# Joint attention products, FFN columns in two halves and a weight conversion divided anew between VectorE and GpSimd

## The chip, the cores and the metric

The kernel runs on one core of a Trainium2 chip. A core has a matrix engine (TensorE), three engines for elementwise work (VectorE, ScalarE, GpSimd; the profile calls them DVE, ACT and POOL), a queue engine that issues most of the transfers (SyncE, SP), and 16 DMA engines. SBUF is the core's working memory, PSUM the memory that TensorE writes to; both have 128 partitions. The metric is the time of one execution on the device in microseconds. Without the change it is 1402.33 us, the median of three runs (1402.2 to 1406.92).

## The reference

Two parts follow each other. The first is an attention that keeps only scores close to the row's maximum; the second a bilinear feed-forward layer (FFN).

```python
# q, k, v: (8, 8, 576, 64) float32; tau = 0.02
scores = q @ k.T / sqrt(64)
thresh = max(scores, axis=-1) - tau
scores = where(scores >= thresh, scores, -1e9)
attn = exp(scores - max(scores)); attn /= attn.sum(-1) + 1e-9
x = (attn @ v) -> (8 * 576, 8 * 64)       # 4608 tokens of 512 numbers
# w_a, w_b: (512, 1536), w_out: (1536, 512), handed over as float64
out = ((x @ w_a) * (x @ w_b)) @ w_out      # float32
```

The three weight matrices arrive as 8-byte floats. The chip computes here in 4-byte floats, so the kernel has to convert them itself.

## The kernel before

**Attention.** Two heads of one batch form a pair; there are 32 pairs, four to a batch, with the first head in partitions 0 to 63 and the second in 64 to 127. A pair's 576 query rows are four units of 128 rows and a remainder of 64; the remainders of two pairs make a unit of their own, so there are 144 units. The main loop (L1117) passes once per unit: such a pass is called a *slot*, with number g, and the first 16 or so differ from the rest. In slot g the kernel computes the scores of unit g on TensorE (`scores`, L404), takes the row maximum (L411) and the threshold (L412) on VectorE, the exponentials on ScalarE (`weigh`, L431 and L432), then on VectorE the *mask*: one instruction that compares, multiplies and sums (L435). The weights must then be turned, keys into partitions. The first eight units (`BY_PE`) are turned on TensorE by a product with a diagonal matrix (`turn_pe`, L483), which also divides by the row sum; ScalarE and VectorE copy the result out of PSUM (L485, L486). Later units are divided by ScalarE (L454), transposed in blocks by VectorE (`turn_blocks`, L502) and regrouped through DRAM by transfers (L144). The product with v (`product`, L546) follows two slots later for the first eight units (`weighted_unit`) and in wider parts for later ones. The first eight units belong to the four pairs of batch 0: units 0 to 3 are the first 128 rows of pairs 0 to 3, units 4 to 7 their second 128 rows.

`product` makes, for one pair, four quarter tiles of 64x64 in `pv`, one per combination of head and half of the columns, with 64 columns moving at a time. `settle` copies them into the tile xT, where partitions hold the 128 features of a pair: one copy by ScalarE (L553), two by VectorE (L554). `exchange` then makes xS on GpSimd (L569), which is xT with the two partition halves swapped, since the FFN's weights are stored so that both are read.

**Weights.** 36 pieces of 128x512 weights are loaded as pairs of 32-bit words (`load_weights`, L271) and converted over the first 16 slots, two or three a slot (`early`, L1113: three in slots 4 to 9). Per piece: ScalarE takes the absolute value of the upper word into the final place (`top`, L298) and prepares the lower word as a number near 2 (`low`, L299); GpSimd clamps `top` (L305); one slot later VectorE puts the sign bit of the upper word into `low` (L311) and shifts `top` left by three (L319); GpSimd adds both as integers (L324). `convert_rest(g, k)` does the last three steps for the k-th piece of slot g - 1, with k = 0 ahead of `weigh`, 1 and 2 near the end of the slot.

**FFN.** The tokens form 18 blocks of 256. `ffn` is a generator that gives out matmuls (L854 and L990 while weights are converted; later a scheme with fewer products, L750 and L920). `advance(cols)` draws from it until that many columns are issued; how many per slot is set by `pace` from fixed shares and from the backlog. Up to slot 8 all of a slot's FFN columns are issued at one place, behind `turn_pe`; from slot 9 on they are issued in four portions.

**Order.** Nothing is reordered: `keep_order` keeps each engine's instructions in the order in which the program issues them. All PSUM tiles come from one pool of four (`banks`), so a new tile waits until the oldest is free; a score tile is free when its mask (L435) is done. The loads of weights use a few rooms in turn and wait for one to be free, and for the last matmul issued before them (`behind`).

Of the kernel before, what the change touches and what calls it, by code (L numbers as in the profile page):

```python
# [23 lines left out]
BY_PE = 8  # L24
# [30 lines left out]
def kernel(  # L55
# [246 lines left out]
    def convert_clamp(n):  # L302
        if n in stages:
            top = pieces[n][0]
            nc.gpsimd.tensor_scalar(top, top, float_of(0x47EFFFFF), float_of(0x38000000),  # L305
                                    op0=ALU.min, op1=ALU.max)

    def convert_sign(n):
        if n in stages:
            low, hi = stages[n].bitcast(U32), raws.pop(n)[:, :, 1]  # L310
            nc.vector.scalar_tensor_tensor(out=low, in0=hi, scalar=0x80000000, in1=low,  # L311
                                           op0=ALU.bitwise_and, op1=ALU.bitwise_or)
            if n in taken:
                extra.append(taken.pop(n))

    def convert_shift(n):
        if n in stages:
            top = pieces[n][0].bitcast(U32)
            nc.vector.tensor_scalar(top, top, 3, None, op0=ALU.logical_shift_left)  # L319
# [152 lines left out]
    def turn_pe(i, u):  # L472
# [4 lines left out]
        turned[i, u, "pe"] = [wT[:, :, y * D:(y + 1) * D] for y in range(2)]  # L477
# [116 lines left out]
    def weighted_unit(i, u):  # L594

        b, hp = pairs[i]
        wT = turned.pop((i, u, "pe"))
        pv = product([lambda rows, s, t=t: t[rows, s] for t in wT], loaded[i]["v"], P)
        settled_of[i] = settled_of.get(i, 0) + P
# [3 lines left out]
        settle(x_of[b, 0][:, hp, u * P:(u + 1) * P], pv, 0, D, ([], []))  # L603
        exchange(x_of[b, 0], state["xs"], hp, u * P, (u + 1) * P, nc.gpsimd)
        if hp == HP - 1:
            state["rows"] = u + 1
            if u == 0:
                blocks.append(((x_of[b, 0], state["xs"]), ("first", b, 0)))
# [10 lines left out]
    def weighted_tails(i):  # L619
# [4 lines left out]
        pv = banks(TAIL, "pv")  # L624
        for s in range(NSLOT):
            for j in range(2):
                rows = slice(j * D, (j + 1) * D)
                for c in range(2):
                    nc.tensor.matmul(pv[c * D:(c + 1) * D, j], loaded[i + c]["v"][rows, s],
                                     t[rows, 2 * c:2 * c + 2, s], start=(s == 0), stop=(s == NSLOT - 1))  # L630
# [474 lines left out]
    def convert_rest(g, k):  # L1105

        for n in early.get(g - 1, [])[k:k + 1]:
            convert_sign(n)
            convert_shift(n)
# [7 lines left out]
    for g in range(len(units) + PV_LAG):  # L1117
# [24 lines left out]
        if 2 <= g < BY_PE + 2:  # L1142
            weighted_unit(*units[g - 2])
# [3 lines left out]
        convert_rest(g, 0)  # L1147
# [13 lines left out]
        for p in range(HP, NPR):  # L1161
            for name, d in (("q0", 1), ("q1", 1)):
                if g == (second if name == "q1" else first)[p] - d - (name == "q1" and p % 2):
                    prep(p, name)
        if here and g < BY_PE:
            reciprocal(i, u, nc.vector)
        if g < 3:
            kT, tp = prep_pe(g + 1, "k")
            nc.scalar.copy(kT.rearrange("p (c k) -> p c k", c=2), tp)
# [112 lines left out]
```

## Time and profile before

| | |
|---|---|
| median of three runs | 1402.33 us |
| profiled execution | 1400.57 us |
| its span, first to last instruction | 1398.8 us |
| mean granted TensorE clock | 0.998 |
| busy in the span: TensorE, VectorE, ScalarE, GpSimd | 97%, 72%, 49%, 35% |
| moved by DMA | 223.21 MB, 160 GB/s on average |
| 36 sign instructions L311 | 26.3 us in all |
| 36 shifts L319 | 22.4 us in all |
| 36 clamps L305 | 23.2 us in all |

A share is busy time over the span. A stage row gives start and end in us from the span's start, its length, then for each engine the busy time and, in brackets, the number of instructions; then the granted clock of TensorE, the share of the DMA engines' time and GB/s. A row of the timeline gives start, length, engine, line and operation, output <- input, shapes. A row of the chain gives start, length and what. In the matmul counts of the records, one matmul of the program is two records.

### The profile page before, as it was taken

How to read it: one execution, taken by the hardware profiler on the slowest of the kernel's cores; microseconds unless marked ns; L12 is line 12 of the kernel's file. 1: busy time of each engine (PE TensorE's matmuls, PEld its weight loads, DVE VectorE, ACT ScalarE, POOL GpSimd, SP SyncE). 2: the span in 40 equal slices, each digit the busy share in tenths (PEclk: the TensorE clock that was granted, in tenths of full speed). 3: DMA queues.
4: the chain of work that ended last, by engine and by line, in shares of the span. 5: the costliest groups of instructions: out<-in, count | busy, mean ns of one | idle time of the engine just before them, and what ended most of it. 6: DMA issues, size and time to landing. Idle time of an engine off the chain costs nothing.

```text
span 1398.8 us, 76307 instructions
## 1 busy us (share of the span) xinstructions
PE 1361.5 (97%) x33836; PEld 1258.5 (90%) x33836; DVE 1013.9 (72%) x2205; ACT 680.8 (49%) x1248; POOL 492.8 (35%) x675
## 2 busy tenths in 40 slices
PE   7889999999999999999999999999999999999998
PEld 5677588999998799999999999998899998799998
DVE  6999877787777768786767776778777776745425
ACT  6977555545554555544454545454545455431110
POOL 2764543424150607060515142332515060708100
PEclk9999999999999999999999999999999999999999
DMA  9977876667666775676556775566656775550000
GB/s 211 241 212 223 204 206 173 174 170 187 174 154 168 190 192 155 176 190 160 143 143 160 186 180 159 136 190 169 181 130 161 199 190 154 137 146 19 4 19 18
DMA packets 327449, 223.21 MB, mean 160 GB/s; under 512 B 171600, under 2 KB 311632, under 8 KB 327120
## 3 DMA queue, kind: packets, MB, share of 16 engines
q1 hardware_dynamic: 323936, 216.95, 60.1%
q8 instruction: 266, 4.36, 1.3%
q10 hardware_dynamic: 3184, 1.38, 0.4%
q14 instruction: 63, 0.52, 0.1%
HBM read 128.58 MB, written 89.65 MB: 156 GB/s over the span
## 4 chain that ended last, share of the span: by engine, by line
PE 88%; DMA 5%; DVE 4%; SPq 2%; issue 1%; ACT 1%; ACTq 0%; DVEq 0%
PE pab L750 29%; PE po L920 22%; PE pab L854 18%; PE sc L404 9%; PE pv L546 9%; SPq L144 1%; DMA vm<-in_v_dram 1%; DMA wT<-swap 1%; DVE tw L435 1%; DVE mx L411 1%; DMA more_u<-in_moe_w_a_dram 1%; DVE low L311 0%; DMA more_u<-in_moe_w_b_dram 0%; DVE tw L502 0%; DMA sums_u<-in_k_dram 0%
## 5 line engine op out<-in xcount | busy, mean ns | idle before, releaser
L454 ACT ACTIVATE tw<-tw,rcp 128x576 f32<-128x576 f32 x272 | 196.1, 768 | 201.3 <-DVE rcp L448 201.3
L411 DVE TENSOR_REDUCE mx<-sc 128x1 f32<-128x576 f32 x288 | 204.6, 752 | 121.2 <-PE sc L404 120.9
L432 ACT ACTIVATE tw<-sc,bias,scalars 128x576 f32<-128x576 f32 x288 | 239.6, 832 | 10.4 <-DMA qT<-in_q_dram 0.4
L712 POOL TENSOR_TENSOR h<-h,u 128x512 f32<-128x512 f32 x28 | 35.2, 1277 | 590.4 <-DVE h L824 414.1
L435 DVE SCALAR_TENSOR_TENSOR tw<-sc,thr,tw 128x576 f32<-128x576 f32 x288 | 220.9, 797 | 12.3 <-ACT tw L432 11.9
L920 PE MATMUL po<-wo_sb,h 64*64 64x256 f32 (+1 forms) x3408 | 210.5, 367 | 0.0
L502 DVE STREAM_TRANSPOSE tw<-tw 128x576 f32<-128x576 f32 x272 | 194.4, 752 | 0.8 <-ACT tw L454 0.8
L920 PEld LDWEIGHTS po<-wo_sb,h 64*64 64x64 f32 x3408 | 169.8, 133 | 14.9
L404 PE MATMUL sc<-kT,qT 64*64 64x288 f32 x2016 | 170.3, 404 | 1.8 <-issue 0.9
L546 PE MATMUL pv<-wT,vm 64*64 64x128 f32 (+2 forms) x4896 | 164.0, 275 | 3.7 <-DMA vm<-in_v_dram 1.4
L546 PEld LDWEIGHTS pv<-wT,vm 64*64 64x64 f32 x4896 | 153.2, 133 | 12.0 <-issue 4.0
L920 PE MATMUL po<-sums_u,h 64*64 64x256 f32 x2448 | 156.6, 376 | 0.0
L883 POOL TENSOR_TENSOR h<-h 128x256 f32<-128x256 f32 x168 | 117.2, 731 | 110.9 <-PE po L920 106.1
L750 PE MATMUL pab<-xU,wb_sb 64*64 64x128 f32 x4352 | 137.8, 269 | 0.0
L920 PEld LDWEIGHTS po<-sums_u,h 64*64 64x64 f32 x2448 | 126.1, 133 | 12.3 <-DVE h L862 0.5
L750 PEld LDWEIGHTS pab<-xU,wb_sb 64*64 64x64 f32 x4352 | 133.3, 133 | 1.8 <-ACT h L806 0.5
L404 PEld LDWEIGHTS sc<-kT,qT 64*64 64x64 f32 x2016 | 108.8, 133 | 17.3 <-issue 4.9
L431 ACT ACTIVATE bias<-mx,scalars 128x1 f32<-128x1 f32 x288 | 82.7, 287 | 66.1 <-DVE mx L411 65.6
L553 ACT COPY xT<-pv 128x128 f32<-128x128 f32 (+1 forms) x68 | 17.6, 259 | 193.5 <-PE pv L546 193.5
L750 PE MATMUL pab<-xS,wa_sb 64*64 64x128 f32 x2176 | 108.5, 269 | 0.8 <-issue 0.8
L554 DVE COPY xT<-pv 64x128 f32<-64x128 f32 (+1 forms) x136 | 38.1, 280 | 80.5 <-PE pv L546 79.0
L535 ACT COPY kept<-po 128x512 f32<-128x512 f32 x65 | 34.8, 535 | 120.3 <-PE po L920 106.4
(163 smaller groups left out, 2468.7 us busy)
## 6 DMA issues: line engine op xcount, KB each, us to landing
wT<-swap SPq DMA_DIRECT2D x242, 288.0 KB, 3.8
swap<-tw SPq DMA_DIRECT2D x480, 144.0 KB, 3.1
vm<-in_v_dram SPq DMA_DIRECT2D x128, 72.0 KB, 2.6
swap<-tw SPq DMA_DIRECT2D x128, 72.0 KB, 2.9
kT<-in_k_dram SPq DMA_DIRECT2D x112, 72.0 KB, 3.2
wT<-swap SPq DMA_DIRECT2D x56, 144.0 KB, 3.6
out_dram<-kept SPq DMA_DIRECT2D x27, 256.0 KB, 3.7
qT<-in_q_dram SPq DMA_DIRECT2D x112, 40.0 KB, 2.8
```

The lines of the kernel that those rows point to most:

```text
L404: nc.tensor.matmul(sc[m][o * D:o * D + wide, c], qT[r, q0:q0 + wide], kT[r, c * SH:(c + 1) * SH], start=True, stop=True)
L411: nc.vector.tensor_reduce(mx[:, c], sc[j], axis=AX.XY, op=ALU.max)
L431: nc.scalar.activation(bias[:, j:j + 1], mx[:, j:j + 1], AF.Copy, scale=e_nscale)
L432: nc.scalar.activation(wb[j], sb[j], AF.Exp, bias=bias[:, j:j + 1], scale=e_scale)
L435: nc.vector.scalar_tensor_tensor(out=wv, in0=sb[j], scalar=thr[:, j:j + 1], in1=wv, op0=ALU.is_ge, op1=ALU.mult, accum_out=sums[:, j:j + 1])
L454: nc.scalar.activation(w, w, AF.Copy, scale=rcp[:, j:j + 1])
L502: nc.vector.transpose(w, w)
L546: nc.tensor.matmul(pv[c * D:(c + 1) * D, y], vm[rows, s], wT[y](rows, s), start=(s == 0), stop=(s == NSLOT - 1))
L750: nc.tensor.matmul(out[c * D:(c + 1) * D, r, f * P:(f + 1) * P], w[g][k][rows, w0:w0 + D], moving[k][rows], start=(fresh and k == 0 and f ...
L854: nc.tensor.matmul(pab[c:c + columns(), r], w[rows, f // n, k, fs + c:fs + c + columns()], moving, start=(k == 0), stop=(k == H - 1))
L883: (nc.vector if state["over"] else nc.gpsimd).tensor_tensor(*a, **kw)
L920: nc.tensor.matmul(po[c * D:(c + 1) * D, r, y, cut], ht[rows, t0:t0 + D], other[rows, f, cut], start=(f == 0), stop=(f == NF // 2 - 1))
```

## The change

Four things are done.

1. *Conversion.* GpSimd, behind each clamp, multiplies the upper word in place by 0.0, read as a float: what is left is a zero with the sign of the weight. VectorE then shifts `top` and joins the sign to it by exclusive-or in one instruction. `low` no longer takes part in this; `convert_shift` is gone.
2. *Joint products.* `weighted_unit` becomes `weighted_units`: in slots 3, 5, 7 and 9 it computes the products of two neighbouring pairs together, with 128 columns moving at a time, in the form that the remainders used already (`by_pairs`, taken out of `weighted_tails`). The copies out of PSUM are those of `tails`: per two units two by ScalarE and two by VectorE, 64x128 each; GpSimd exchanges two pairs in one copy.
3. *FFN columns.* Up to slot 8 half of a slot's columns is issued ahead of `turn_pe` and half at the place before.
4. *Place of the first conversion.* From slot 9 on `convert_rest(g, 0)` comes behind `turn_blocks` and `weigh` instead of ahead of them.

```diff
             nc.gpsimd.tensor_scalar(top, top, float_of(0x47EFFFFF), float_of(0x38000000),
                                     op0=ALU.min, op1=ALU.max)
+            hi = raws[n][:, :, 1].bitcast(FP32)
+            nc.gpsimd.tensor_scalar(hi, hi, 0.0, None, op0=ALU.mult)
 
     def convert_sign(n):
         if n in stages:
-            low, hi = stages[n].bitcast(U32), raws.pop(n)[:, :, 1]
-            nc.vector.scalar_tensor_tensor(out=low, in0=hi, scalar=0x80000000, in1=low,
-                                           op0=ALU.bitwise_and, op1=ALU.bitwise_or)
+            top, sign = pieces[n][0].bitcast(U32), raws.pop(n)[:, :, 1]
+            nc.vector.scalar_tensor_tensor(out=top, in0=top, scalar=3, in1=sign,
+                                           op0=ALU.logical_shift_left, op1=ALU.bitwise_xor)
...
-    def convert_shift(n):
-        if n in stages:
-            top = pieces[n][0].bitcast(U32)
-            nc.vector.tensor_scalar(top, top, 3, None, op0=ALU.logical_shift_left)
...
-    def weighted_unit(i, u):
+    def weighted_units(i, u):
 
         b, hp = pairs[i]
-        wT = turned.pop((i, u, "pe"))
-        pv = product([lambda rows, s, t=t: t[rows, s] for t in wT], loaded[i]["v"], P)
+        wT = [turned.pop((i + c, u, "pe")) for c in range(2)]
+        pv = by_pairs(P, i, lambda rows, c, s: wT[c][rows, s])
...
-        settle(x_of[b, 0][:, hp, u * P:(u + 1) * P], pv, 0, D, ([], []))
-        exchange(x_of[b, 0], state["xs"], hp, u * P, (u + 1) * P, nc.gpsimd)
+        x, xs, cols = x_of[b, 0], state["xs"], slice(u * P, (u + 1) * P)
+        tails(x, pv, hp, cols.start, cols.stop)
+        for r in range(2):
+            nc.gpsimd.tensor_copy(xs[r * D:(r + 1) * D, hp:hp + 2, cols], x[(1 - r) * D:(2 - r) * D, hp:hp + 2, cols])
...
+    def by_pairs(n, i, moving):
+
+        pv = banks(n, "pv")
+        for s in range(NSLOT):
+            for j in range(2):
+                rows = slice(j * D, (j + 1) * D)
+                for c in range(2):
+                    nc.tensor.matmul(pv[c * D:(c + 1) * D, j], loaded[i + c]["v"][rows, s], moving(rows, c, s),
+                                     start=(s == 0), stop=(s == NSLOT - 1))
+        return pv
...
         if 2 <= g < BY_PE + 2:
-            weighted_unit(*units[g - 2])
+            if g % 2:
+                weighted_units(*units[g - 3])
             running["owed"] -= NSLOT * P // 2
...
-        convert_rest(g, 0)
+        if g <= BY_PE:
+            convert_rest(g, 0)
...
+        if g > BY_PE:
+            convert_rest(g, 0)
...
+        if g <= BY_PE:
+            advance(pace / 2)
         if 0 < g <= BY_PE:
             turn_pe(*units[g - 1])
...
         if g <= BY_PE:
-            advance(pace)
+            advance(pace / 2)
```

## The prediction

> **What bounds the kernel now.** I read the page first (busy shares, then the 40 slices), then the busy times by stage, then the early part instruction by instruction on VectorE and GpSimd, then the chain that ended last and the waits there.
>
> ```profile
> PE 1361.5 (97%) x33836; PEld 1258.5 (90%) x33836; DVE 1013.9 (72%) x2205; ACT 680.8 (49%) x1248; POOL 492.8 (35%) x675
> PE   7889999999999999999999999999999999999998
> DVE  6999877787777768786767776778777776745425
> POOL 2764543424150607060515142332515060708100
> ```
>
> TensorE is full over nearly the whole span, but not in the first four slices of 35 us, where VectorE is. A slot is one pass of the main loop; I cut the early part where the threshold instruction L412 starts in slots 1, 5, 11, 16 and 22. The rows give busy time per engine, granted clock and the share of the DMA engines.
>
> ```profile
> 17.60:47.45 29.85, 25.76 (x492) 21.26 (x493) 26.66 (x64) 24.73 (x52) 17.41 (x22) 1.00 1.16 223
> 47.45:104.28 56.83, 47.06 (x890) 42.17 (x886) 54.20 (x111) 47.33 (x96) 41.72 (x48) 0.97 0.85 227
> 104.28:142.75 38.47, 35.93 (x528) 29.60 (x530) 37.04 (x82) 29.75 (x60) 18.48 (x21) 1.00 0.81 225
> 142.75:183.40 40.65, 38.17 (x621) 25.36 (x617) 36.18 (x81) 23.43 (x44) 24.69 (x19) 1.00 0.82 202
> 183.40:1398.80 1215.40, 1204.21 (x31275) 1132.36 (x31267) 852.95 (x1851) 547.48 (x985) 388.53 (x562) 1.00 0.58 151
> ```
>
> After 183.4 us TensorE is busy 1204.21 of 1215.40 us (99.1%); nothing the change does reaches it, and each slot still issues the same matmul work. So a microsecond won while weights are converted is won at the end. Slots 5 to 10 finish three pieces each, VectorE 95.4% busy; slots 11 to 15 finish two, VectorE 96.3%, TensorE 93.4%. In slots 1 to 4 the DMA share is 1.16, the highest here, and the chain goes mostly through transfers (vm 8.52 us, more_u 8.15 us). The chain inside slots 5 to 10 goes through VectorE, the shift L319 in it:
>
> ```profile
> 53.08 0.75 DVE wb_sb L319
> 53.83 0.60 DVE low L311
> 54.43 1.43 DVE wa_sb L319
> 55.86 1.34 DVE mx L411 x2
> ```
>
> Why a shift takes 0.4 us once and 1.5 us another time is seen by laying GpSimd (last two lines, its int add) beside VectorE:
>
> ```profile
> 53.75 0.68 DVE L311 SCALAR_TENSOR_TENSOR low<-more_u,low 128x512 uint32<-128x512 uint32 x1
> 54.35 1.50 DVE L319 TENSOR_SCALAR wa_sb<-wa_sb 128x512 uint32<-128x512 uint32 x1
> ...
> 53.92 1.66 POOL L324 TENSOR_TENSOR wb_sb<-wb_sb,more_u 128x512 int32<-128x512 int32 x1 [0.36 <-DVE wb_sb L319]
> 55.94 1.26 POOL L324 TENSOR_TENSOR wa_sb<-wa_sb,low 128x512 int32<-128x512 int32 x1 [0.36 <-DVE wa_sb L319]
> ```
>
> The add was stretched from 1.26 to 1.66 us while the sign instruction L311 ran, and the shift ended 0.27 us after that add: the two engines keep each other out. Durations (min/median/max ns), and in the last line a wait of TensorE for a mask (us in all, times, longest):
>
> ```profile
> L319 DVE TENSOR_SCALAR wa_sb<-wa_sb x12: 413/512/1515, 19.0 to 91.9; 128x512 uint32<-128x512 uint32 x12
> L311 DVE SCALAR_TENSOR_TENSOR low<-raw,low x15: 669/682/1664, 18.4 to 131.6; 128x512 uint32<-128x512 uint32 x15
> L305 POOL TENSOR_SCALAR wa_sb<-wa_sb x12: 612/614/902, 14.4 to 84.4; 128x512 f32<-128x512 f32 x12
> L324 POOL TENSOR_TENSOR wa_sb<-wa_sb,low x10: 1259/1272/1704, 19.5 to 93.5; 128x512 int32<-128x512 int32 x10
> PE pab L854 <- DVE tw L435: 5.9, 5, 1.6
> ```
>
> **The change part by part.** The profiled execution took 1400.57 us (span 1398.8 and 1.8 around it); the median of the runs is 1.76 above it, 1402.33.
>
> *Shift and sign in one, sign by GpSimd, slots 5 to 10.* 36 shifts go, 22.4 us by stage: 4.0, 14.2 and 4.2. The new instruction has the form of L311 (two tensors, 128x512), so I price it as L311, 0.68, with nothing to add. GpSimd gets 36 multiplies. The trace has none on every second word; bounds are its one-input clamp (0.614) and its two-input add (1.27). I take the clamp's, the same operation on as many words. VectorE falls from 54.20 to 40.0 us. GpSimd rises by 18 x 0.614 = 11.1 from 41.72; its exchanges fall from 5.36 us (five units) to three pairs of two copies, by the 64x256 row 0.395 alone or some 0.67 when stretched like the 64x128 ones (0.30 alone, 0.51 on average): 2.4 to 4.0, taken 3.2. That leaves GpSimd at 50.6 us, above ScalarE's unchanged 47.33 and TensorE's 47.06. Held as full as VectorE was (95.4%), GpSimd makes the stage 53.0 us: 3.8 won. Ends: 14.2 won (all shifts) and 8.6 lost (multiply at 1.27, below).
>
> The Trainium skill (GPSIMD Engine Reference, 7. Performance pitfalls for Q7 kernels) has GpSimd's reads slow down by half once the step exceeds 8 bytes. Here the step is exactly 8, so by it the multiply keeps the clamp's price; were it past the step (0.92, an estimate from the clamp), the stage would be 59 us, 2 longer than before. No run here shows it yet.
>
> What queues there: the multiply stands behind its clamp and ahead of the next int add, and the sign now waits for it too. It is the next slot's work, so a delay of 0.61 is covered until GpSimd is full; then the adds, and behind them TensorE's reading of weights, come late.
>
> *Slots 11 to 15.* VectorE falls from 37.04 to 32.9, GpSimd rises from 18.48 to 24.6, ScalarE stays 29.75; TensorE's 35.93 is next. At the 99.1% it has later, 36.3: 2.2 won at most, 0 at least; I take 2.0, as no other engine is within 3 us.
>
> *Slots 1 to 4.* VectorE loses 4.0 of 26.66 us, but transfers lead: 0 to 2 won, taken 0.5.
>
> *FFN columns in two halves, up to slot 8.* Before, the four slots 5 to 8 issue them all behind the transposes, whose buffers wait for the masks (tw L435); 5.9 us of TensorE's waits are that. At 53.74 the next scores start only after 48 matmul records, some 2.8 us, behind such a wait. Half of them now stand ahead: up to 1.4 us less in each of four slots, 5.6; the other way, the first half of slot 5 may wait for the copies to xT, which now come after both units' products: 1.3 us lost (as GpSimd's wait for xT in this stretch). Taken 2.0 won, as the other bounds leave little more.
>
> *Joint products.* Eight units of 72 records of 64 columns (11.1 us in all, 19.3 ns each) become four of 72 of 128 columns (33.6 ns each by the later rows: 9.7 us): 1.4 us less on TensorE. VectorE has 16 copies of 0.22 before and 8 of 0.29 after, 1.2 us less. The pair's first unit is consumed one slot later, but the last unit, for which the FFN waits, in the same slot. Hidden below the bounds above: 0, between -1 and 1.4.
>
> *Conversion behind masks, slots 9 to 15.* It puts 1.1 us of VectorE work behind the two transposes and the masks. So the transposed tiles leave SyncE's queue earlier (it waits 13.9 us for L502 in all) while the raw buffer's next load, also issued by SyncE, comes some 3 us later (1.43 + 1.55), within a slot of 7 to 9. Taken 0, between -1 and 1.
>
> Sum: 3.8 + 2.0 + 0.5 + 2.0 = 8.3, so 1400.57 - 8.3 = 1392.3 for a profiled execution and **1394.0** for the median.
>
> **The rivals.**
> - *The waits move rather than go.* Of the shifts' 22.4 us, 36 x 0.41 = 14.8 is work and 7.6 is waiting for GpSimd. The new instruction is of a form that waits too (L311 at 71.88 took 1.66 us, ending 0.54 after an add), and GpSimd is busier. Then VectorE in slots 5 to 10 goes to 46.9 us plus what the added multiplies hold it up, 18 x 0.31 = 5.5: 52.4, a gain of 1.8; with 2 from slots 11 to 15, 1398.5. For it: every such wait above. Against: two signs in a row leave GpSimd no gap to enter. The Trainium skill (GPSIMD Engine Reference, 8. Key points) says that GpSimd shares its SBUF interfaces with VectorE and collides with instructions of two SBUF inputs as well as those in a two-port mode; by that rule this rival is right, and the trace agrees (1.66 us against 0.68).
> - *TensorE becomes the bound everywhere.* Its idle time in slots 1 to 15 is 125.15 - 108.75 = 16.4 us; all of it and the 1.4 of the products gone gives 1384.5. Half the distance from the forecast, 1388, is this case's middle. Against: transfers in slots 1 to 4, GpSimd after that.
> - *GpSimd becomes a worse bound: slower.* With a multiply at 1.27 us, GpSimd has 39.5 + 22.9 = 62.4 us in slots 5 to 10; at 95.4% the stage is 65.4, 8.6 longer; less 2.0 from slots 11 to 15, 1409. It decides from 0.92 us a multiply on, where the stage loses 2; 0.5% is lost from about 1.3 us. For it: no row with this stride, and clamps stretched to 0.90. Against: the clamp's median.
>
> **How the numbers follow.** The forecast's case (gain 5 to 11) 0.48, waits that move 0.26, TensorE everywhere 0.16, GpSimd worse 0.10. About 0.5%, 7 us, is what a measurement can tell from no change; 1395.3 is that line. Faster: four fifths of the first and all of the third, 0.55. Slower: most of the last, 0.08. Same: 0.37. The range: low 1383, just past the TensorE bound; high 1403, past the moved waits and the cheap end of the last rival.
>
> **What would show it.** Right: no L319; 36 multiplies near 0.61 us; VectorE below 85% and GpSimd above 92% between the thresholds of slots 5 and 11, that stretch near 51 us (53.0 less 2.0); the one for slots 11 to 15 near 36.5 with TensorE at 98%. The second rival is right if TensorE is above 95% from slot 5 on; the first if the new sign averages over 1.0 us. Wrong: multiplies near 1.2 us, or a stage after 183 us longer than 1215 us.

## The result, and the profile after

The change made the kernel slower: 1419.8 us (median of four runs, 1417.13 to 1421.95) against 1402.42 us beside it on the same chip, a ratio of 1.0115 with a 95% interval of 1.0092 to 1.0138. The forecast was 1394.0, with 1383 to 1403 as its range. The profiled execution took 1421.09 us, 20.5 more than that of before. First the page's busy line and slices.

```profile
PE 1371.0 (97%) x33548; PEld 1272.1 (90%) x33548; DVE 1003.7 (71%) x2161; ACT 681.4 (48%) x1248; POOL 549.7 (39%) x703
PE   6778999999999999999999999999999999999998
DVE  5778976788777877786757767677777776745425
POOL 4999840706060514233242415150606060608100
```

GpSimd, which had 2, 7, 6, 4 and 5 tenths in the first slices, now has 4, 9, 9, 9 and 8: it is full from 35 to 140 us, and VectorE, fullest there before, no longer is. The same stages as before, cut where the threshold (now L409) starts in slots 1, 5, 11, 16 and 22; the last row is all that follows:

```profile
17.76:51.23 33.47, 23.66 (x304) 19.22 (x307) 25.61 (x52) 25.92 (x53) 26.84 (x24) 0.86 1.15 225
51.23:120.28 69.05, 53.46 (x800) 47.05 (x792) 49.31 (x89) 47.22 (x96) 68.43 (x60) 0.92 0.73 191
120.28:158.72 38.44, 37.14 (x516) 31.83 (x520) 35.23 (x72) 29.61 (x60) 37.30 (x32) 0.91 0.73 197
158.72:203.00 44.28, 39.86 (x621) 26.90 (x617) 36.30 (x81) 23.44 (x44) 24.93 (x20) 0.96 0.79 199
203.00:1419.30 1216.30, 1206.51 (x31275) 1139.33 (x31267) 850.38 (x1851) 547.14 (x985) 388.29 (x562) 1.00 0.57 150
```

Slots 1 to 4 take 3.6 us more than before, slots 5 to 10 take 12.2 more, slots 11 to 15 the same, slots 16 to 21 3.6 more, the rest 0.9 and the part ahead of slot 1 0.2: together the 20.5. In slots 5 to 10 GpSimd is busy 68.43 of 69.05 us, 99%. Of the 3.6 us more in slots 16 to 21, 3.1 stand at one place, a product that waited 2.50 us for its transposed tile (1.09 before) and then took 3.75 us in place of 2.08; why that transfer was late I did not follow up.

The rows of the multiply's line, durations as min/median/max in ns, show what fills GpSimd:

```profile
L308 POOL TENSOR_SCALAR raw<-raw x19: 1535/1559/2045, 15.1 to 153.4; 128x512 f32<-128x512 f32 x19
L308 POOL TENSOR_SCALAR sums_u<-sums_u x9: 1548/1572/2071, 61.1 to 138.8; 128x512 f32<-128x512 f32 x9
L308 POOL TENSOR_SCALAR more_u<-more_u x8: 1562/1582/2033, 34.2 to 146.3; 128x512 f32<-128x512 f32 x8
```

The 36 multiplies take 59.2 us (31.0, 14.7 and 13.5 by the groups of the page), 1.64 each, where the forecast had 0.614 and its upper bound was 1.27. What that does to the others is seen in the timeline of VectorE in slot 8:

```profile
83.33 0.71 DVE L409 TENSOR_SCALAR thr<-mx,scalars 128x2 f32<-128x2 f32 x1
86.13 1.74 DVE L313 SCALAR_TENSOR_TENSOR wb_sb<-wb_sb,raw 128x512 uint32<-128x512 uint32 x1 [2.09 <-POOL raw L308]
87.80 0.81 DVE L432 SCALAR_TENSOR_TENSOR tw<-sc,thr,tw 128x576 f32<-128x576 f32 x1
```

In the timeline of GpSimd of the same kernel, at the same time:

```profile
84.56 1.53 POOL L308 TENSOR_SCALAR raw<-raw 128x512 f32<-128x512 f32 x1
86.07 1.26 POOL L321 TENSOR_TENSOR wb_sb<-wb_sb,low 128x512 int32<-128x512 int32 x1
```

And in that of TensorE:

```profile
88.76 0.70 PE L480 MATMUL tp<-first_u,tw 128*64 128x128 f32 x4 [6.53 <-DVE tw L432]
```

VectorE idles 2.09 us until the multiply ends. Its new sign instruction then takes 1.74 us and ends 0.5 us after the add that GpSimd runs beside it (alone such an instruction takes 0.68); the mask stands behind it, and TensorE, which turns the mask's result, stands still for 6.53 us. Then TensorE's granted clock is lower: 0.75 over this slot (83.33 to 96.81 us), where the kernel of before had 0.83 in its slot 8 (75.25 to 85.35). So part of a stall is paid for a second time, in slower matmuls.

### The profile page after: what moved, and what is told of

Read it like the earlier page. It is cut to its first block, busy times and chain, and to the rows that moved or that the text cites. A ratio compares the mean times of both kernels' runs of the same rounds, so it can differ in the third digit from the quotient of the medians.

```text
span 1419.3 us, 75743 instructions
## 1 busy us (share of the span) xinstructions
PE 1371.0 (97%) x33548; PEld 1272.1 (90%) x33548; DVE 1003.7 (71%) x2161; ACT 681.4 (48%) x1248; POOL 549.7 (39%) x703
## 4 chain that ended last, share of the span: by engine, by line
PE 89%; POOL 4%; DMA 2%; SPq 1%; DVE 1%; issue 1%; ACT 1%; POOLq 0%; DVEq 0%; ACTq 0%
PE pab L755 30%; PE po L925 22%; PE pab L859 18%; PE sc L401 10%; PE pv L543 9%; POOL raw L308 1%; POOL wb_sb L321 1%; DMA wT<-swap 1%; POOL sums_u L308 1%; SPq L198 1%; POOL wa_sb L321 1%; PE pv L617 1%; POOL more_u L308 0%; PE po L995 0%; DMA sums_u<-in_k_dram 0%
## 5 line engine op out<-in xcount | busy, mean ns | idle before, releaser
L925 PE MATMUL po<-wo_sb,h 64*64 64x256 f32 (+1 forms) x3408 | 213.9, 367 | 0.0
L925 PEld LDWEIGHTS po<-wo_sb,h 64*64 64x64 f32 x3408 | 173.4, 133 | 13.2
L401 PE MATMUL sc<-kT,qT 64*64 64x288 f32 x2016 | 173.5, 404 | 2.3 <-issue 1.8
L543 PE MATMUL pv<-wT,vm 64*64 64x128 f32 (+1 forms) x4320 | 156.8, 284 | 3.3 <-DMA wT<-swap 2.5
L543 PEld LDWEIGHTS pv<-wT,vm 64*64 64x64 f32 x4320 | 146.5, 134 | 8.4 <-issue 3.8
L755 PE MATMUL pab<-xS,wa_sb 64*64 64x128 f32 x2176 | 111.9, 269 | 0.3 <-issue 0.3
L550 ACT COPY xT<-pv 128x128 f32<-128x128 f32 x60 | 15.9, 265 | 196.8 <-PE pv L543 196.8
L755 PE MATMUL pab<-xT,wa_sb 64*64 64x128 f32 x1856 | 94.6, 269 | 0.0
L755 PEld LDWEIGHTS pab<-xS,wa_sb 64*64 64x64 f32 x2176 | 93.4, 133 | 1.3 <-issue 1.0
```

Source lines behind the costliest of these rows:

```text
L401: nc.tensor.matmul(sc[m][o * D:o * D + wide, c], qT[r, q0:q0 + wide], kT[r, c * SH:(c + 1) * SH], start=True, stop=True)
L543: nc.tensor.matmul(pv[c * D:(c + 1) * D, y], vm[rows, s], wT[y](rows, s), start=(s == 0), stop=(s == NSLOT - 1))
L755: nc.tensor.matmul(out[c * D:(c + 1) * D, r, f * P:(f + 1) * P], w[g][k][rows, w0:w0 + D], moving[k][rows], start=(fresh and k == 0 and f ...
L925: nc.tensor.matmul(po[c * D:(c + 1) * D, r, y, cut], ht[rows, t0:t0 + D], other[rows, f, cut], start=(f == 0), stop=(f == NF // 2 - 1))
```

## The experiments

The chips of these runs took 1408 to 1411 us for the kernel of before, so only ratios to it are compared; positions by slot are against before's trace from the first chip, and each comes from one profile. Where two kernels do the same they still scatter: e7, which is the kernel of before up to slot 8, starts slot 2 1.9 us earlier than before and slot 8 3.2 us later. The stage of slots 5 to 10 can be checked with e8, which is the kernel of before behind a few probes:

```profile
48.01:103.05 55.04, 46.61 (x900) 41.81 (x898) 54.18 (x111) 46.49 (x95) 41.96 (x48) 0.99 0.88 231
```

That is 1.8 us shorter than before's 56.83 with the same work; before has 3.4 us at half the clock in this stage, and e8 only its first 1.3. So a difference of less than 2 us between single stages is no finding.

The first question was why the multiply is dear. Theories: the step of two words in what it reads, the step in what it writes, or something in the operation itself. The second was what of the loss belongs to the other three parts.

### e1: the multiply with no step at all

```diff
-            nc.gpsimd.tensor_scalar(hi, hi, 0.0, None, op0=ALU.mult)
+            dense = raws[n].rearrange("p f w -> p (f w)")[:, 0:CW].bitcast(FP32)
+            nc.gpsimd.tensor_scalar(dense, top, 0.0, None, op0=ALU.mult)
```

> The changed kernel, but GpSimd's multiply reads the clamped contiguous words and writes contiguous words (the first 512 of the raw buffer), and VectorE takes those as the sign. Left out: the sign, so all weights are positive. Same count of instructions on every engine. Theory A (the price of the multiply at a step of two words is what costs): a multiply near 0.61 us instead of 1.56, GpSimd about 51 us busy in slots 5 to 10, whole time 1388 to 1398 us, as forecast. Theory B (the other parts, joint products, halves or order, cost the time): multiply near 0.61 us too, but the time stays above 1410 us. Theory C (VectorE's new instruction waits for GpSimd wherever it stands): new instruction still about 1.05 us on average and the time within 3 us of 1402.

Ratio 1.0144 (1.0123 to 1.0166). The multiply reads the clamped magnitude and writes contiguous words, and still takes 1.56 us on average (56.2 us for 36). None of the expected times came true, since the price did not move: the step is not the cause.

### e4: the multiply writes contiguous words, but reads every second

```diff
-            nc.gpsimd.tensor_scalar(hi, hi, 0.0, None, op0=ALU.mult)
+            dense = raws[n].rearrange("p f w -> p (f w)")[:, 0:CW].bitcast(FP32)
+            nc.gpsimd.tensor_scalar(dense, hi, 0.0, None, op0=ALU.mult)
```

> The changed kernel, the multiply reads every second word as before but writes contiguous words, which VectorE then reads. Nothing is left out. If the step of the reads is what costs: a multiply still near 1.5 us and a time of 1414 to 1422 us. If the step of the writes is what costs: a multiply near 0.61 us and 1388 to 1398 us. If both share it: near 1.1 us and about 1400 to 1406 us.

Ratio 1.0124 (1.0102 to 1.0147); the multiplies average 1.60 us (57.7 us for 36). Between e1 (1.56) and the change (1.64) the step is worth less than 0.1 us.

### e8: the price of the multiply, by itself

```diff
+    room = more_sb[:, 0:2 * CW]
+    two = room.rearrange("p (f w) -> p f w", w=2)[:, :, 1]
+    one, other = room[:, 0:CW], more_sb[:, CW:2 * CW]
+    nc.gpsimd.memset(room, 0.5)
+    for _ in range(2):
+        nc.gpsimd.tensor_scalar(one, one, 2.0, 0.25, op0=ALU.min, op1=ALU.max)
+        nc.gpsimd.tensor_scalar(two, two, 2.0, 0.25, op0=ALU.min, op1=ALU.max)
+        nc.gpsimd.tensor_scalar(one, one, 1.0, None, op0=ALU.mult)
+        nc.gpsimd.tensor_scalar(one, one, 1.0, 1.0, op0=ALU.mult, op1=ALU.mult)
+        nc.gpsimd.tensor_scalar(one, one, 2.0, None, op0=ALU.min)
+        nc.gpsimd.tensor_scalar(two, two, 1.0, None, op0=ALU.mult)
+        nc.gpsimd.tensor_scalar(two, two, 0.0, None, op0=ALU.mult)
```

> The kernel before with fourteen GpSimd instructions on 128x512 words of an unused room while GpSimd has nothing to do: twice each a clamp (min, max) dense and at a step of two words, a multiply by 1.0 dense, two multiplies in one dense, a min alone dense, a multiply by 1.0 and one by 0.0 at a step of two words. If the operation multiply is what costs: clamps and the min near 0.61 us, all multiplies near 1.5. If an instruction with one operation costs more than one with two: the min alone near 1.5 and the two multiplies in one near 0.61. If the value 0.0 costs: only the last near 1.5.

The kernel of before with probes at its start; the rows are the first of the two rounds, in which VectorE has little to do (its first instruction starts at 6.33 us). The timeline of GpSimd gives, in the order of the diff:

```profile
2.27 0.61 POOL L356 TENSOR_SCALAR more_u<-more_u 128x512 f32<-128x512 f32 x1
2.97 0.64 POOL L357 TENSOR_SCALAR more_u<-more_u 128x512 f32<-128x512 f32 x1
3.69 1.49 POOL L358 TENSOR_SCALAR more_u<-more_u 128x512 f32<-128x512 f32 x1
5.26 0.62 POOL L359 TENSOR_SCALAR more_u<-more_u 128x512 f32<-128x512 f32 x1
5.97 1.49 POOL L360 TENSOR_SCALAR more_u<-more_u 128x512 f32<-128x512 f32 x1
7.54 1.58 POOL L361 TENSOR_SCALAR more_u<-more_u 128x512 f32<-128x512 f32 x1
9.20 1.55 POOL L362 TENSOR_SCALAR more_u<-more_u 128x512 f32<-128x512 f32 x1
```

Two operations in one instruction take 0.61 to 0.64 us, whether minimum and maximum or two products (L356, L357, L359). One operation alone takes 1.49, whether a product or a minimum (L358, L360). A step of two words adds 0.03 us to the one kind and 0.09 to the other (L357, L361), and the value 0.0 adds nothing (L362). So the instruction with *fewer* operations costs 2.4 times as much, and the clamp, which has two, was no price for a multiply with one. The Trainium skill (GPSIMD Engine Reference, 7. Performance pitfalls for Q7 kernels) has reads slow down past a step of 8 bytes; 0.61 against 0.64 at exactly 8 agrees. What makes the form with one operation dear, no run here shows.

### e9 and e10: the same change with two operations

e9 is the changed kernel with one line edited; e10 is the kernel of before with this conversion and nothing else.

```diff
-            nc.gpsimd.tensor_scalar(hi, hi, 0.0, None, op0=ALU.mult)
+            nc.gpsimd.tensor_scalar(hi, hi, 0.0, 1.0, op0=ALU.mult, op1=ALU.mult)
```

> The changed kernel with the multiply written with two operations (by 0.0, then by 1.0), all else alike. The multiply should fall from 1.6 to 0.62 us, GpSimd in slots 5 to 10 from 99% to near 90%. If the price of the multiply is all that the forecast had wrong, 0.992 to 0.997 of before. If the other three parts keep the cost they had alone (e2: 1.0083), the conversion's gain of 6.3 us by the forecast's terms (0.9955) leaves 1.002 to 1.006.

> The kernel before with the new conversion alone and the multiply written with two operations. By the forecast's terms for the conversion (3.8, 2.0 and 0.5 us): 0.993 to 0.998 of before. If the waits for GpSimd move to the new instruction instead: 0.997 to 1.001, the new instruction at 1.0 us or more on average. If it is still slower than before by 0.3% or more, the price of the multiply was not what made the conversion slow.

e9: 1.0016 (0.9999 to 1.0034), multiplies 0.725 us on average (26.1 us for 36). e10: 1.0004 (0.9984 to 1.0024). The dear form was thus worth about 1% of the whole kernel's 1.15%. But the kernel is not faster than before either: e9 came out just below what its second expectation had (1.002 to 1.006), and e10 as in its second, though with a sign of 0.90 us and not 1.0 or more. VectorE was relieved by less than half of what was planned. Slots 5 to 10 of e10:

```profile
48.39:106.25 57.86, 47.67 (x896) 42.88 (x898) 47.81 (x92) 46.40 (x96) 53.94 (x64) 0.96 0.81 211
```

VectorE fell from 54.20 to 47.81 us, where the forecast had 40.0; GpSimd rose from 41.72 to 53.94 and is 93% busy, and the stage is 1.0 us longer than before's 56.83, which is within the scatter.

### e3: the conversion of the change alone

The kernel of before with the conversion as the change has it (the first two hunks of the diff and no `convert_shift`), nothing else.

```diff
+            hi = raws[n][:, :, 1].bitcast(FP32)
+            nc.gpsimd.tensor_scalar(hi, hi, 0.0, None, op0=ALU.mult)
...
+            nc.vector.scalar_tensor_tensor(out=top, in0=top, scalar=3, in1=sign,
+                                           op0=ALU.logical_shift_left, op1=ALU.bitwise_xor)
```

> The kernel before with the new conversion alone (multiply on GpSimd, shift and sign in one). Theory A: GpSimd as full as in the changed kernel in slots 5 to 10 (18 multiplies at 1.6 us), so slower by as much or a little more than the changed kernel: 1417 to 1426 us. Theory B: at or below the time before, 1392 to 1402 us.

Ratio 1.0147 (1.0127 to 1.0168): the conversion alone costs at least what the whole change does. It loses 15.8 us between the thresholds of slots 5 and 11, e10 only 1.0. The difference, 14.8, is close to 18 multiplies x (1.64 - 0.78) = 15.5.

### e2: the other three parts with the old conversion

```diff
-            hi = raws[n][:, :, 1].bitcast(FP32)
-            nc.gpsimd.tensor_scalar(hi, hi, 0.0, None, op0=ALU.mult)
...
+            nc.vector.tensor_scalar(top, top, 3, None, op0=ALU.logical_shift_left)
```

> The changed kernel with the conversion of before (sign and shift each on VectorE, no multiply on GpSimd); joint products, halved FFN columns and the later place of the first conversion stay. Theory A: what slowed the kernel is gone; the three parts are worth what the forecast gave them, 0 to 5 us, so 1397 to 1403 us. Theory B: slower than before by 5 us or more, 1407 us and above.

Ratio 1.0083 (1.0057 to 1.0109): these three parts lose as well. In its slot 2 the product that used to stand there is gone, and TensorE has nothing to do until q and then k have come:

```profile
25.39 0.69 PE L378 MATMUL tp<-more_u,sums_u 96*128 96x96 f32 x6 [3.95 <-DMA sums_u<-in_q_dram]
27.55 1.19 PE L378 MATMUL tp<-more_u,sums_u 96*128 96x96 f32 x6 [1.47 <-DMA sums_u<-in_k_dram]
28.67 4.11 PE L483 MATMUL tp<-first_u,tw 128*64 128x128 f32 x36
```

### e5, e6 and e7: each of the three alone

e5 has the joint products, e6 the FFN halves, e7 the conversion behind the masks. The diffs of the latter two are short:

```diff
+        if g <= BY_PE:
+            advance(pace / 2)
...
-            advance(pace)
+            advance(pace / 2)
```

```diff
-        convert_rest(g, 0)
+        if g <= BY_PE:
+            convert_rest(g, 0)
...
+        if g > BY_PE:
+            convert_rest(g, 0)
```

The core of e5's, which is the change's own:

```diff
-            weighted_unit(*units[g - 2])
+            if g % 2:
+                weighted_units(*units[g - 3])
```

> The kernel before with the joint products alone. Theory D (a product that left slot 2 uncovers TensorE's wait for the rows of pair 3, the clock granted to TensorE drops, and slots 4, 6 and 8 have less to fill waits): the threshold of slot 3 comes some 2 us later than before, that of slot 9 at 88 to 90 us instead of 85.35, the whole 3 to 5 us slower. Theory E (the joint products are harmless, the halves did it): both within 1 us of before.

> The kernel before with the FFN columns in two halves alone, up to slot 8. Theory D: threshold of slot 3 as before, slot 9 within 1 us of 85.35 or up to 2 earlier, whole 0 to 2 us faster. Theory E: slot 9 some 4 us later, whole 4 us slower.

> The kernel before with convert_rest(g, 0) behind turn_blocks and weigh from slot 9 on, alone. Theory F (sign and shift behind the masks push the reciprocal L448 back, ScalarE's division L454 and with it the next slot's transposes): slots 9 to 15 each 0.7 to 1.2 us longer, threshold of slot 15 at 139 to 142 us instead of 134.02, whole 5 to 8 us slower. Rival (the lengthening there comes from the later start of those slots alone): within 1.5 us of before at slot 15 and in the whole.

e5: 1.0049 (1.0031 to 1.0067). Neither of its expectations came true: it starts slot 3 0.7 us earlier than before and slot 9 1.9 later, and loses more than 5 us in all. It starts slot 5 0.8 us earlier than before and slot 11 2.5 us later, so it loses 3.3 in between; the rest of its 6.9 us I could not place. e6: 1.0005 (0.9987 to 1.0024), no gain where 2.0 us were forecast. e7: 1.0034 (1.0016 to 1.0051). From slot 9 to slot 15 it falls back from 1.7 to 7.9 us behind, about 1 us a slot. The place is ScalarE's division, in e7:

```profile
113.21 1.44 ACT L454 ACTIVATE tw<-tw,rcp 128x576 f32<-128x576 f32 x2 [0.81 <-DVE rcp L448]
122.41 1.44 ACT L454 ACTIVATE tw<-tw,rcp 128x576 f32<-128x576 f32 x2 [1.04 <-DVE rcp L448]
```

Before has 0.24 and 0.23 there. The moved instructions now stand on VectorE between the masks and the reciprocal, and the division, whose result is transposed and sent off next, waits for that reciprocal. That this wait makes up the whole microsecond a slot is argued from the order of the program; no run takes it out alone. The three alone add up to 0.88%, which is e2's 0.83%.

### e11 and e12: which of the parts still cost with the cheap conversion

e11 is e10 with the FFN halves (the edit of e6); e12 is e9 with the edit of e7 undone.

```diff
-        if g <= BY_PE:
-            convert_rest(g, 0)
+        convert_rest(g, 0)
...
-        if g > BY_PE:
-            convert_rest(g, 0)
```

> As e10_conversion_two_op, and the FFN columns in two halves. If the halves are worth something once VectorE is no longer full (forecast 2.0 us): 0.001 to 0.003 below e10. If they are not (e6: 1.0005): within 0.001 of it.

> As e9_full_two_op, with the first conversion back at the place of before from slot 9 on. If that place costs as it does alone (e7: 1.0034): 0.002 to 0.005 below e9. If it costs nothing once the shift is gone, since a single instruction then stands ahead of the reciprocal: within 0.001 of e9.

e11: 1.0002 (0.9986 to 1.0019). e12: 1.0011 (0.9994 to 1.0028). Beside e10 (1.0004) and e9 (1.0016) nothing can be told apart: with the cheap conversion the three parts, which cost 0.83% with the old one, cost 0.12% by the medians (e9 against e10), with an uncertainty of some 0.3%.

### e13, e14 and e15: why the cheap conversion wins nothing

Two suspects: the new sign instruction waits for GpSimd with the masks behind it (the prediction's first rival), or GpSimd is full. e13 is e11 with one line moved; e14 is e10 without the clamp; e15 is e13 without the clamp.

```diff
-        convert_rest(g, 0)
         if g == 0:
...
+        convert_rest(g, 0)
         if here and g < BY_PE:
             reciprocal(i, u, nc.vector)
```

```diff
-            nc.gpsimd.tensor_scalar(top, top, float_of(0x47EFFFFF), float_of(0x38000000),
-                                    op0=ALU.min, op1=ALU.max)
```

> The kernel of e11 (before, with the two-operation conversion and the ffn halves) with one line moved: the conversion of a slot's first piece of a, b or c stands behind the slot's masks in all slots, not ahead of them. Theory V (the new sign instruction on VectorE waits for GpSimd with the masks queued behind it, and that wait is what takes back the gain that the forecast gave the conversion): the stage between the thresholds of slots 5 and 11 falls from 57.9 us in e10 to 55.5 or less, ratio to before 0.996 to 0.999. Theory G (GpSimd is simply full in that stage, 53.9 of 57.9 us busy in e10, and the order on VectorE does not matter): stage 57 to 58.5 us, ratio within 0.001 of e11's 1.0002. Theory R (the conversion behind the masks stands ahead of the reciprocal and makes ScalarE's division wait, as e7 showed with the old instructions): 1.002 to 1.006, with ScalarE's divisions waiting near 1 us for the reciprocal.

> The kernel of e10 (before, with the two-operation conversion alone) without the clamp of the magnitude: this leaves out the limiting of very small and very large weights, so GpSimd does two instructions for a piece in the place of three, 0.61 us less each, 36 pieces. Theory G (GpSimd full is the bound): its busy time in the stage of slots 5 to 11 falls by some 12 x 0.61 = 7 us from 53.9 to 47 us, the stage from 57.9 to 54 us or less, ratio 0.994 to 0.998. Theory V (the wait of the sign instruction ahead of the masks): the sign instruction is ready 0.6 us sooner, the stage shrinks by at most 6 x 0.6 = 3.6 us and its waits of about 1 us remain in part: 0.998 to 1.000. A third, that the stage is held by TensorE and VectorE alone: like e10, 0.9995 to 1.0015, with the stage at 57 to 58 us.

> The kernel of e13 without the clamp of the magnitude (the limiting of very small and very large weights is left out): both suspected causes taken away. If the two theories each hold a part, this is the fastest of the three, 0.992 to 0.996, with the stage of slots 5 to 11 at 53 us or less. If only one of them holds, it is within 0.001 of the better of e13 and e14. If the stage is held by TensorE and VectorE alone, it is within 0.001 of e11's 1.0002.

The wait does exist in e10. In its timeline of VectorE:

```profile
76.48 1.74 DVE L313 SCALAR_TENSOR_TENSOR wb_sb<-wb_sb,raw 128x512 uint32<-128x512 uint32 x1 [0.94 <-POOL raw L308]
...
78.15 0.81 DVE L432 SCALAR_TENSOR_TENSOR tw<-sc,thr,tw 128x576 f32<-128x576 f32 x1
```

and in that of GpSimd, whose add from 76.42 on keeps the sign from starting its work:

```profile
75.80 0.65 POOL L308 TENSOR_SCALAR raw<-raw 128x512 f32<-128x512 f32 x1
76.42 1.26 POOL L321 TENSOR_TENSOR wb_sb<-wb_sb,low 128x512 int32<-128x512 int32 x1
```

But taking the masks out from behind it does not help: e13 is 1.003 (1.001 to 1.005). In slots 5 to 8, where only one division has to wait, 0.23 us, its signs wait 0.5 us for GpSimd and e11's 4.2, yet these slots take 36.52 us in e13 and 36.54 in e11. Taking 0.7 us a piece off GpSimd does help: e14 is 0.9938 (0.9916 to 0.996). The busy times by stage, slots 5 to 10, of e13:

```profile
48.72:106.83 58.11, 49.59 (x892) 43.99 (x892) 45.79 (x92) 45.45 (x94) 53.17 (x64) 0.97 0.87 233
```

and of e14:

```profile
46.04:97.12 51.08, 45.83 (x874) 41.36 (x872) 41.71 (x93) 46.18 (x95) 41.78 (x47) 0.97 0.94 246
```

In e13 GpSimd is as busy as in e10 and the stage as long. In e14 GpSimd has 41.78 us, 12.2 less (7 were expected, from 12 pieces where the stage has 18), and the stage is 6.8 us shorter than e10's and 4.0 shorter than e8's; VectorE no longer idles for GpSimd ahead of its sign instructions (5.1 us in e10), and these take 0.72 us on average (26.0 us for 36) against 0.90 in e10. So the expectation of the wait ahead of the masks falls, and that of GpSimd's load is borne out, as far as leaving out the clamp changes nothing but the load; e16 below tests that. e15, 0.9976 (0.9957 to 0.9996), is slower than e14 and faster than e13: behind the masks the conversion costs something with either load, which none of the expectations for e15 had. It has the form of e7's loss: in e13 the division waits up to 1.37 us for the reciprocal, and e13's ratio is what its third expectation had.

### e16: the clamp left out with the old conversion

```diff
-            nc.gpsimd.tensor_scalar(top, top, float_of(0x47EFFFFF), float_of(0x38000000),
-                                    op0=ALU.min, op1=ALU.max)
+            pass
```

> The kernel of before with its own conversion, but without the clamp (the limiting of very small and very large weights is left out). The control for e14 (0.9938): if the clamp's removal helps only because the new conversion fills GpSimd, this is 0.999 to 1.001, as GpSimd is busy 41.7 of 56.8 us between the thresholds of slots 5 and 11 of before and VectorE 54.2. If shortening any piece's chain helps, or the shift's waits for the clamp were what mattered, it is 0.994 to 0.998 like e14.

Ratio 0.9967 (0.9948 to 0.9987), so the clamp's removal is worth something by itself: 0.33%, against 0.66% with the new conversion (e10 to e14). Had only a full GpSimd mattered, this would have been no change. By the medians half of what e14 gained comes without a full GpSimd, and half hangs on it. Slots 5 to 10 take 55.58 us here, between before's and e8's time, with GpSimd busy 29.59 us and VectorE 51.33: VectorE, still the fuller, is busy 2.9 us less (54.20 before).

### e17 and e18: the load divided, with nothing left out

e17 uses the new conversion, with two operations, for one piece of three in slots 5 to 10 and the old one for the other two; e18 for two of three (`in (0,)` in the diff's second line). In all other slots both use the new one.

```diff
+    def by_gpsimd(n):
+        return not (8 <= n < 26 and (n - 8) % 3 in (0, 2))
...
+            if by_gpsimd(n):
+                hi = raws[n][:, :, 1].bitcast(FP32)
+                nc.gpsimd.tensor_scalar(hi, hi, 0.0, 1.0, op0=ALU.mult, op1=ALU.mult)
```

> The kernel of e10 with the new conversion for one piece of three only (the second) in slots 5 to 10, the old conversion for the other two there, and the new one for all pieces of the other slots. Nothing is left out. By the busy times of before and e10 in that stage, GpSimd 41.7 + (53.9 - 41.7) / 3 = 45.8 us, VectorE 54.2 - 6.4 / 3 = 52.1 us. Theory G (whichever of VectorE and GpSimd is fuller holds the stage): the stage falls by about 2 us, ratio 0.997 to 0.9995. Theory V (any sign instruction ahead of the masks that waits for GpSimd loses what it saves): the first piece, ahead of the masks, is the old kind, so the waits go: 0.997 to 0.999 as well. If neither: within 0.001 of 1.

> As e17, but the new conversion for two pieces of three (the second and third) in slots 5 to 10. Nothing is left out. GpSimd 41.7 + 2 x 4.1 = 49.9 us, VectorE 54.2 - 2 x 2.1 = 49.9 us: the most even load. Theory G: the fastest of the versions that leave nothing out, stage about 53 to 55 us, ratio 0.995 to 0.998, and faster than e17. Theory V: like e17, since the first piece is of the old kind in both. If neither: within 0.001 of 1.

e17: 0.997 (0.9953 to 0.9987). e18: 0.9975 (0.9958 to 0.9992). Both beat the kernel of before and the changed one, by little. The busy times by stage, slots 5 to 10, of e17:

```profile
47.86:104.25 56.39, 45.25 (x876) 39.99 (x874) 53.67 (x104) 46.56 (x96) 45.98 (x53) 1.00 0.88 227
```

and of e18:

```profile
49.10:103.25 54.15, 43.25 (x856) 38.44 (x852) 50.34 (x99) 46.21 (x95) 50.51 (x58) 1.00 0.84 219
```

With the even load, 50.34 and 50.51 us, the stage of e18 is 54.15, inside the 53 to 55 expected and 2.2 shorter than e17's, where VectorE still has 53.67. (e17's stage was expected 2 us shorter than before's; it is 0.4.) e18 as a whole is not faster than e17, though, as had been expected: it took 31.39 us in slots 1 to 4 against 30.05, where both kernels do nearly the same. Neither stage had any time at half the clock (1.00 in both rows). Beside e8's 55.04 us, which had hardly any either, e17's stage is 1.4 longer and e18's 0.9 shorter. So the gain of 0.3% in the whole is measured, but that the even load brings it is not shown by these two stages, and which of the two divisions is better stays open.

## Why the prediction was wrong

**The price of the multiply: the step that failed.** Forecast and result, as ratios 0.994 and 1.0115, lie 1.75% apart. About 1.0% is this price (the change against e9); the other 0.75% is that the gains of the sum did not come even with a cheap multiply (e9's 1.0016 against 0.994).

"I take the clamp's, the same operation on as many words" gave 0.614 us, with the two-input add's 1.27 as the upper bound. It measured 1.64. The clamp is not the same kind of operation: it has two, the multiply has one, and e8 puts one at 1.49 and two at 0.62. The bounds came from rows that shared the shape and the number of inputs, and the property that counted was not among them; the step of 8 bytes, on which the working spent its one doubt, was innocent.

**GpSimd as a worse bound: right in its mechanism, too small in its price.** The third rival's own sum, 39.5 us plus 18 multiplies, gives 69.0 us at 1.64 (it had 62.4), and GpSimd was busy 68.43. At 95.4% that is a stage of 72; it came to 69.05, as GpSimd was 99% busy. The rival ended at 1409 us because its price stopped at 1.27, and had 0.10 of the chance.

**Slots 5 to 10 with the right price: 3.8 us won, measured 0.5, which is within the scatter.** e9 is what the forecast described: multiplies at 0.725 us, GpSimd 52.78 us busy where 50.6 were forecast, and the stage 56.32 us (53.0 forecast, 56.83 before). Of the missing 3.3 us, 2.2 are more work on GpSimd than summed (18 multiplies at 0.11 more are 2.0 of it), and the rest is that GpSimd was busy 93.7% of the stage in the place of 95.4%. A second reading failed with it: the working took all 14.2 us of the shifts off VectorE, down to 40.0 us. e9 has 48.62 there and e10 47.81. Of the 7.8 us by which e10 stays above, 4.7 are longer signs: 18 of them took 18.59 us, where those of before had taken 13.87. That a lighter GpSimd shortens the stage is shown by e14, with the reservation that e16 makes; e17 and e18 gain in the whole but not clearly in this stage.

**Waits that move: seen, and not decisive.** The new sign averages 1.06 us in the changed kernel (38.0 us for 36) and waits another 15.7 for the multiply; in e10 it averages 0.90 and waits 5.1. The Trainium skill (GPSIMD Engine Reference, 8. Key points) has GpSimd share its SBUF interfaces with VectorE and contend with its instructions of two SBUF inputs; the traces agree, with 1.74 us beside an add against 0.68. Some 0.36 us are lost on a piece in e10 (0.22 of length, 0.14 of waiting), where the rival had 0.31, and e9's and e10's outcome, no change, is nearer to its 1398.5 than to 1394.0. Its 46.9 us for VectorE, before the added 5.5, was far nearer to what e10 shows (47.81) than the forecast's 40.0. By the sign that the prediction gave for it, a new sign of over 1.0 us on average, it would be right in the changed kernel. But e13 shows that the place of the wait is not what holds the stage.

**Slots 11 to 15: 2.0 won, measured 0 to 0.8.** The stage is 38.44 us in the changed kernel, 37.70 in e10 and 38.05 in e9, against 38.47. In e14, where VectorE has 34.56 and GpSimd 21.32 us in it, it is still 38.03. No engine's busy time alone was the bound there, and "TensorE at 99.1%" is not reached by relieving one: it was 96% in e14.

**Slots 1 to 4: 0.5 won.** 29.85 us before; in the versions with the cheap conversion between 28.27 (e14) and 32.22 (e15), with no order by GpSimd's or VectorE's load. e7 and e8, which are the kernel of before in these slots, took 31.06 and 31.40: the scatter is larger than the term. Transfers lead there, as the working said.

**FFN halves: 2.0 won, measured none** (e6, 1.0005). The wait did go, from 5.9 us to 2.1, but others took its place. TensorE's longest waits of e6 up to 143 us (us in all, times, longest):

```profile
PE tp L378 <- DVE wa_sb L319: 2.1, 1, 2.1
PE pab L854 <- DVE tw L435: 2.1, 3, 1.1
...
PE pab L854 <- DVE xT L554: 1.4, 1, 1.4
```

The first and the last are not among the nine longest of before; the last is the loss that the working priced at 1.3. VectorE is as full as before, and TensorE stands ready earlier only to wait for it at another place.

**Joint products, between -1 and 1.4: a loss of 0.49%** (e5), some 7 us, and **conversion behind the masks, between -1 and 1: a loss of 0.34%** (e7), some 5 us. The second was costed for the transposes and the loads in SyncE's queue; it puts 1.1 us of VectorE ahead of the reciprocal for which ScalarE waits, and the working did not name that. For the first the cause is not settled: the wait for q that e2 shows in slot 2 cannot be all, since e5 starts slot 5 no later than before, and loses in slots 5 to 10. All three parts together hardly cost anything with the cheap conversion (e9 against e10, 0.12%), which suggests that they were losses mainly where VectorE was full.

**The rest of the span.** The work after slot 22 took 1216.30 us against 1215.40, nearly as forecast (the working allowed 1215). What it left out is the clock: within the first 203 us the granted clock was 0.86 to 0.96 by stage, where the rows of before say 0.97 to 1.00. (The 1.00 of before's slots 1 to 4 is too high, see below.) In the second rival, half the distance from 1394.0 to 1384.5 is 1389.3 and not 1388; nothing hangs on it.

## What to carry to other kernels

Price an added instruction from a row that agrees in engine, shape *and form* (how many operations, how many inputs); where no row does, the bound is open upward, and a probe of a dozen lines settles it. Moving work from a full engine to a free one can move too much: here one or two pieces in three gave 0.3%, and all of them nothing. Work that waits for the other engine does not vanish when it is taken off a list; its waits turn up in the instruction that is left. An instruction put between a producer and its small follow-up (here a reciprocal) is paid for by the engine that waits for the follow-up.

## What the runs showed of the hardware

- GpSimd's instruction with a tensor and constants took 1.49 us with one operation and 0.62 with two, on 128x512 four-byte floats (e8). Writing a needless product by 1.0 into the second place cut the multiply from 1.64 to 0.725 us in the kernel (e9). A step of two words cost 0.03 to 0.09 us.
- TensorE was granted half its clock for some microseconds around long waits. The busy times by stretch of the changed kernel, at the wait of 6.53 us shown above:

```profile
85.00:90.00 5.00, 1.24 (x10) 0.94 (x12) 3.58 (x7) 4.19 (x9) 5.00 (x5) 0.60 0.03 11
```

  In e2, 36 records of the turning product took 4.11 us behind waits of 3.95 and 1.47 us; at 58.16 us of e10, with the full clock, as many took 2.34. (The granted clock of e2 from 25 to 30 us was 0.61.) The Trainium skill (TensorE: Matmul & The Clock Gate, Part 1: The HAM clock gate) puts the clock back to half after an idle window of about 3.4 us; the waits of 6.53 and 3.95 us are that long.
- Short waits were followed by half the clock as well, but not always. In slot 8 of before TensorE was granted 0.50 from 78.5 to 81.5 us:

```profile
76.47 0.44 PE L483 MATMUL tp<-first_u,tw 128*64 128x128 f32 x4 [0.96 <-DVE xT L554]
78.36 2.08 PE L854 MATMUL pab<-xT,wa_sb 64*128 64x128 f32 x16 [1.45 <-DVE tw L435]
```

  At the same place of e8, behind waits of 1.03 and 1.45 us, the same 16 records took 1.16 us. So the length of a wait does not tell by itself whether the clock falls; what decides it, these runs do not show.
- Early in the span, a clock of 1.00 in a row need not mean full speed. In before 36 records of the turning product took 4.11 us at 18.64 us, in a stage whose row says 1.00; in e2 as many took 2.19 at 17.89. The trace of before has no record of the clock that early.
- The share of the DMA engines in the row from 85 to 90 us is 0.03. The queue that issues the loads of weights waits there, 5.5 us for a sign instruction and 5.2 us for a matmul: when the conversion stalls, so do the loads behind it.
